# Causal mask added in the row maximum instead of by a matrix product, and small additions moved to GpSimd

## The chip, the cores and the metric

One core of a Trainium2 chip runs the whole kernel. The metric is the time on the device in microseconds (us), as the median of several executions. The engines work side by side, each through a queue of its own in order: TensorE (PE) multiplies matrices and writes to PSUM, VectorE (DVE) and ScalarE (ACT) read and write PSUM and SBUF, GpSimd (POOL) works on SBUF alone, and SyncE (SP) issues DMAs.

## What is computed

Causal attention over 2 batches and 12 heads of 448 positions and 64 dimensions, then a dense layer with squared ReLU, then a layer of 8 experts of which each token uses one. The change is in the attention:

```python
scores = scale * np.matmul(q, k.transpose(0, 1, 3, 2))
mask = np.triu(np.ones((seq, seq), dtype=bool), k=1)
scores = np.where(mask, -1000000000.0, scores)
scores = scores - np.max(scores, axis=-1, keepdims=True)
attn = np.exp(scores)
attn = attn / (np.sum(attn, axis=-1, keepdims=True) + 1e-09)
return np.matmul(attn, v).astype(np.float32)
```

## The kernel before

Attention works on 12 units, each a pair of heads of one batch. A unit's 448 queries are cut into 7 chunks of 64; a score tile holds the chunk's 64 queries of both heads on its 128 partitions, and the n = (c + 1) x 64 keys up to the chunk's end as columns, so that only its last 64 columns (QC) need a mask. There are 84 such tiles.

For each tile `s_scores` issues three products on PE (line 215; the operands are split into a high and a low part, kh and kl, q likewise) into one of four PSUM banks, then a fourth one (line 216): the identity matrix times `mask`, a tile of 0 and -1e9 in bf16, accumulated on the last 64 columns. Then DVE takes the negated row maximum `mn` (line 218), and ACT computes p = exp(s + mn) with the row sums `sm` as a by-product (line 219). The bank is free again when ACT has read it.

`s_norm` runs twice for each unit, for 4 chunks and for 3: DVE adds 1e-9 to the row sums (line 225) and takes the reciprocal `rs` (line 226), and POOL multiplies p by it (line 230). `s_trans` then transposes p on PE (line 247), ACT rounds the result to its high part (line 250, in the helper on line 59) and DVE subtracts to get the low part (line 251, in the helper on line 66). `s_pv` multiplies with v (line 264), and `s_x` stores the sum as xhi (ACT) and xlo (DVE). `s_prep` splits q and k of a later unit, and moves q into place with two DMAs from SP's queue (line 191).

The units run as a software pipeline: two steps for each unit, whose order of work is written out in `seq` (s is scores, n is norm, t is transpose, v is the product with v, p and w prepare a later unit). The tile framework turns that into a queue for each engine, ordered by a simulated timeline, and adds the semaphore waits; so a change of one instruction can shift others in their queues. In the first microseconds POOL fills the constants and clears the padding (lines 75 to 80, 145 to 151). Behind attention comes phase A (lines 288 to 290), the first dense layer, with 16 weight tiles that are loaded and converted by DVE, POOL and ACT on the way; the load of the first three hangs on the last row maximum issued so far (`last["max"]`).

Of the kernel before, what the change touches and what calls it, by code (L numbers as in the profile page):

```python
# [8 lines left out]
F32 = mybir.dt.float32  # L9
# [3 lines left out]
AF = mybir.ActivationFunctionType  # L13
ALU = mybir.AluOpType
AX = mybir.AxisListType
PSUM = bass.MemoryType.PSUM

B, H, S, D = 2, 12, 448, 64
NT, DM, FF = 896, 768, 2048
E, F = 8, 1024  # L20
P = 128
NP_ = H // 2
QC = 64
# [9 lines left out]
def f32(ap):  # L33
    return ap.bitcast(F32)


CFG = dict(
    first=1, rt5=[1, 3, 4, 5, 8], hp=3000, xe=[1, 10, 11, 12, 13], turn=5, xfd=[3, 4, 5, 6], xfj=[1, 2, 3, 4],
    joint=1, mhi="A", rt6=[1, 4, 7, 9, 15], woh="A", h2h="A", h2l="V", rt=[1, 3, 5, 7, 10], et=[9, 10, 14],
    turn2=[1, 3], ft0=[0, 1, 2, 3, 4], ft1=[3], ft2=[2, 4, 5, 6], ew=[2, 4, 10, 10, 10, 12, 14], stop=0, mlo="V", xh="A", h2="A",  # L40
    wh="G", wil="G", wol="GV", warm=6, nsa=6, nwi=3, nwb=3, wo0=4, hs0=[4, 5, 8, 9], conv0=17, convs=2, pin=1,
    qsb=2, pb=2, ptb=2, qkraw=3, vraw=2, vb=2, ss=4, pts=3, pvs=1, pas=4, wsp=1, mz="G",
    seq=("p0 s0 n0 t0 v0 s1 v1 s2 t1", "n0 t2 s0 v2 v3 t3 s1 s2 w0"),
    ch=(((2, 0, 1), (3,), ()), ((6,), (4, 5), ())), wn=[1], qh="A", qdir=1, qss=2, rpin=5, qdma="SS", kh="V",
    vh="AG", kl="G", vl="G", pth="AAAA", nrm="GGGGGGG", u0=1, order=[2, 1, 3, 0, 4])


def build(tc, qkd, vd, w_in, w_out, emb, tau, wm, cst, out, dbg_y=None):
    nc = tc.nc
    V, A, G, T, DMA = nc.vector, nc.scalar, nc.gpsimd, nc.tensor, nc.sync  # L50
# [20 lines left out]
    identb = cpool.tile([P, P], BF16, name="identb")  # L71
    V.tensor_copy(identb, ident)

    mask = cpool.tile([P, QC], BF16, name="mask")
# [54 lines left out]
    last = {}  # L129
    apool = tc.alloc_tile_pool(name="attn", bufs=1, side="right")  # L130
# [4 lines left out]
    units = [(b, pr) for b in range(B) for pr in range(NP_)]  # L135
# [8 lines left out]
    for i in range(Z):  # L144
# [5 lines left out]
        for x in vz[i] if i < len(vz) else ():  # L150
            ENG[CFG["mz"]].memset(f32(x[:, :, 1]), 0.0)

    def ab(key, u):
        x = CFG[key]
        return ENG[x[units.index(u) % len(x)]]
# [13 lines left out]
    def s_prep(u):  # L169

        d = st[u]
        for x in ("kh", "kl"):
            d[x] = apool.tile([P, S], F32R, tag=x, bufs=CFG["qsb"], name=x)
        d["q2"] = qz[units.index(u) % len(qz)]
        first = u == units[0] and CFG["u0"]
        copy_on(V if first else ab("kh", u), d["kh"], d["k"])

        def split(r, hi, lo):
            q = d["q"][r].rearrange("p (c a) -> p c a", a=QC)
            copy_on(ENG[CFG["qh"]], hi, q, scale=SCALE)  # L180
            V.scalar_tensor_tensor(out=lo, in0=q, scalar=SCALE, in1=f32(hi), op0=ALU.mult, op1=ALU.subtract)

        heads = [slice(h * D, (h + 1) * D) for h in range(2)]
        if units.index(u) < CFG["qdir"]:
            for h, r in enumerate(heads):
                split(r, d["q2"][r, :, h, :, 0], d["q2"][r, :, h, :, 1])
        else:
            q = apool.tile([P, NQ, QC, 2], F32R, tag="qs", bufs=CFG["qss"], name="qs")
            split(slice(0, P), q[:, :, :, 0], q[:, :, :, 1])
            for h, r in enumerate(heads):  # L190
                ENG[CFG["qdma"][h]].dma_start(out=f32(d["q2"][r, :, h]), in_=f32(q[r]))
        lo_of(V if first else ab("kl", u), d["kl"], d["k"], f32(d["kh"]))

    def s_prep_v(u):
        d = st[u]
        d["vh"], d["vl"] = vz[units.index(u) % len(vz)]
        vh, vl = (x[:, :, 0:3:2, :] for x in (d["vh"], d["vl"]))
        v = d["v"].rearrange("p a (h b) -> p a h b", h=2)
        copy_on(ab("vh", u), vh, v)
        lo_of(V if u == units[0] and CFG["u0"] else ab("vl", u), vl, v, f32(vh))  # L200
# [4 lines left out]
    def s_scores(u, c):  # L205

        d = st[u]
        if "p" not in d:
            for x in ("sm", "mn", "rs"):
                d[x] = apool.tile([P, NQ], F32, tag=x, bufs=3, name=x)  # L210
            d["p"] = pz[units.index(u) % len(pz)]
        n = (c + 1) * QC
        ss = ps_s.tile([P, 512], F32, tag="s", name="s")[:, 0:n]
        for i, (x, y) in enumerate(((0, "kh"), (0, "kl"), (1, "kh"))):
            T.matmul(ss, d["q2"][:, c, :, :, x].rearrange("p a b -> p (a b)"), d[y][:, :n], start=i == 0, stop=False)  # L215
        T.matmul(ss[:, n - QC:n], identb, mask, start=False, stop=True)  # L216
        i = COL[c]
        last["max"] = V.reduce_max(out=d["mn"][:, i:i + 1], in_=ss, axis=AX.X, negate=True)  # L218
        A.activation(d["p"][c][:, :n], ss, AF.Exp, bias=d["mn"][:, i:i + 1], accum_out=d["sm"][:, i:i + 1])  # L219

    def s_norm(u, cs):
        d = st[u]
        rs = d["rs"]
        x = slice(COL[cs[0]], COL[cs[-1]] + 1)
        V.tensor_scalar(out=rs[:, x], in0=d["sm"][:, x], scalar1=1.0e-9, scalar2=None, op0=ALU.add)
        V.reciprocal(rs[:, x], rs[:, x])
        for c in cs:
            p = d["p"][c][:, :(c + 1) * QC]
            if CFG["nrm"][c] == "G":
                G.tensor_scalar(out=p, in0=p, scalar1=rs[:, COL[c]:COL[c] + 1], scalar2=1.0, op0=ALU.mult, op1=ALU.mult)  # L230
            else:
                V.tensor_scalar(out=p, in0=p, scalar1=rs[:, COL[c]:COL[c] + 1], scalar2=None, op0=ALU.mult)
# [82 lines left out]
    def norm_at(k):  # L315
        u = (k + 2) // 2
        if 0 <= u < NU:
            s_norm(units[u], sum(CFG["ch"][k % 2], ()))
# [16 lines left out]
    for k in range(-3, 2 * NU + 2):  # L335
        u, h = divmod(k, 2)
        if h == 0 and -1 <= u and u + 3 < NU:
            s_load(units[u + 3])
        while len(wt) < min(NWI, max(0, (k - CFG["conv0"]) // CFG["convs"])):
            if CFG["pin"]:  # L340
                with tc.issue_after(last["max"].ins):
                    w_in_load()
            else:
                w_in_load()
        sc = scores_at(k)
        for x in CFG["seq"][h].split():
            i = int(x[1])
            if x[0] == "p" and -1 <= u and u + 2 < NU:
                s_prep(units[u + 2])
            if x[0] == "w" and 0 <= u + 1 < NU:  # L350
                s_prep_v(units[u + 1])
            if x[0] == "n":
                norm_at(k)
            if x[0] == "t" and 0 <= u < NU:
                s_trans(units[u], i)
            if x[0] == "v" and u >= 1:
                s_pv(units[u - 1], i)
                if i == NB - 1:
                    s_x(units[u - 1])
            if x[0] == "s":  # L360
                for y in sc[i]:
                    s_scores(*y)
                if k + 3 < len(CFG["wn"]):
                    warm(CFG["wn"][k + 3])
# [540 lines left out]
    y = ys[NTI - 1]  # L905
# [274 lines left out]
```

## Time and profile before

| | us |
|---|---|
| median of 3 runs | 587.28 |
| the runs | 587.99, 587.28, 583.95 |
| the profiled execution | 583.95 |
| its span, first to last instruction | 582.2 |

The profiled execution is the fastest of the three. PE is busy for 96% of the span and DVE for 69%. Rows give starts and durations; durations of neighbours on one engine overlap, so that the price of an instruction to its engine is read from start to start.

### The profile page before, as it was taken

To read this page: it belongs to the slowest core of one execution; us is meant where nothing else is said; L and a number is where in the kernel's file an instruction comes from. 1 tells how busy PE (TensorE), PEld (TensorE's weight loads), DVE (VectorE), ACT (ScalarE), POOL (GpSimd) and SP (SyncE) were. 2 spreads that over 40 slices of the span, in tenths; PEclk is the share of its full clock that TensorE was granted. 3 is DMA by queue.
4 is the path that set the end of the run, shared out by engine and by line. 5 is a ranking of instruction groups with operands and counts; after the bars stand their busy time and mean duration, and the time that the engine had idled before them with its cause. 6 is when DMAs were issued, how large, how long until landed. Compare 5 with 4: busy or idle time off the path is not lost.

```text
span 582.2 us, 9781 instructions
## 1 busy us (share of the span) xinstructions
PE 558.6 (96%) x3501; PEld 512.2 (88%) x3501; DVE 399.6 (69%) x901; ACT 291.5 (50%) x654; POOL 188.3 (32%) x204
## 2 busy tenths in 40 slices
PE   6999999999999999999999999899998999899994
PEld 3888788889999999999999999799997888799993
DVE  6878688955777878597664376975387986932641
ACT  4768678523343433434333226721478877923651
POOL 7676667854445544221000001001203412500010
PEclk8899999999999999999999999999999999899998
DMA  7757542223444655351000009404887987950310
GB/s 222 176 145 230 125 100 70 84 81 110 156 148 142 204 177 184 130 179 70 23 28 28 1 28 377 164 3 149 306 254 239 339 329 237 337 176 29 110 49 5
DMA packets 28233, 86.51 MB, mean 149 GB/s; under 512 B 2822, under 2 KB 13062, under 8 KB 28176
## 3 DMA queue, kind: packets, MB, share of 16 engines
q1 hardware_dynamic: 26640, 79.51, 42.3%
q0 software_dynamic: 1536, 6.29, 2.9%
q8 instruction: 29, 0.48, 0.3%
q14 instruction: 28, 0.23, 0.1%
HBM read 75.24 MB, written 6.29 MB: 140 GB/s over the span
## 4 chain that ended last, share of the span: by engine, by line
PE 85%; DVE 5%; DMA 4%; ACT 3%; issue 2%; SPq 1%; POOL 0%; POOLq 0%; ACTq 0%
PE yps L500 19%; PE ops L797 10%; PE pa L290 7%; PE pa L289 7%; PE pa L288 7%; PE pv L264 6%; PE s L215 5%; PE pt L247 3%; PE hps L707 3%; DMA q<-qs 3%; PE ops L739 3%; PE ops L734 2%; DVE ml L66 2%; PE hps L723 2%; PE hps L722 2%
## 5 line engine op out<-in xcount | busy, mean ns | idle before, releaser
L66 DVE TENSOR_TENSOR ml<-xraw,mh 128x768 fp32r<-128x768 f32 x64 | 60.1, 953 | 15.4 <-ACT mh L59 15.3
L59 ACT ACTIVATE mh<-xraw 128x768 fp32r<-128x768 f32 x64 | 53.3, 845 | 18.8 <-PE ops L734 9.3
L215 PE MATMUL s<-kh,q 128*128 128x128 f32 (+6 forms) x168 | 53.5, 352 | 4.3 <-ACT p L219 4.3
L797 PE MATMUL ops<-mh,act 128*128 128x384 f32 x224 | 53.5, 341 | 0.0
L819 POOL DMA_INDIRECT out<-osb,fsi x10 | 24.3, 2432 | 88.9 <-ACT osb L814 63.8
L230 POOL TENSOR_SCALAR p<-p,rs 128x192 f32<-128x192 f32 (+6 forms) x84 | 44.2, 545 | 17.9 <-ACT p L219 11.0
L264 PE MATMUL pv<-pt,v 128*128 128x448 f32 (+7 forms) x288 | 48.6, 303 | 0.2 <-DVE pt L66 0.2
L219 ACT ACTIVATE p<-s,mn 128x192 f32<-128x192 f32 (+6 forms) x84 | 39.5, 475 | 10.9 <-DVE mn L218 7.0
L123 DVE SCALAR_TENSOR_TENSOR w<-raw,w 128x768 int32<-128x768 int32 x32 | 42.8, 1339 | 0.7
L264 PEld LDWEIGHTS pv<-pt,v 128*128 128x128 f32 (+3 forms) x288 | 36.9, 163 | 5.4 <-issue 0.3
L215 PEld LDWEIGHTS s<-kh,q 128*128 128x128 f32 x168 | 35.5, 215 | 6.2 <-ACT p L219 4.9
L797 PEld LDWEIGHTS ops<-mh,act 128*128 128x128 f32 x224 | 39.2, 188 | 0.8
L66 DVE TENSOR_TENSOR ml<-mraw,mh 128x768 fp32r<-128x768 f32 x32 | 30.1, 953 | 14.3 <-ACT mh L59 14.3
L831 POOL DMA_INDIRECT xr<-ydram,fgi x10 | 10.7, 1067 | 89.3 <-DVE fsi L609 47.1
L66 DVE TENSOR_TENSOR hs<-h,hs 128x512 fp32r<-128x512 f32 (+1 forms) x32 | 21.9, 691 | 24.6 <-ACT hs L59 24.4
L218 DVE TENSOR_REDUCE mn<-s 128x1 f32<-128x192 f32 (+6 forms) x84 | 34.3, 415 | 5.7 <-PE s L216 5.5
L121 DVE SCALAR_TENSOR_TENSOR w<-raw,w 128x768 int32<-128x768 int32 x32 | 36.0, 1127 | 0.7
L294 ACT ACTIVATE relu<-pa 128x448 f32<-128x448 f32 x32 | 17.1, 537 | 36.3 <-PE pa L290 36.3
L119 DVE TENSOR_SCALAR w<-raw 128x768 int32<-128x768 int32 x32 | 22.2, 694 | 18.7 <-POOL wi3l L66 6.7
L66 DVE TENSOR_TENSOR pt<-pt 128x512 fp32r<-128x512 f32 x48 | 32.4, 680 | 3.1 <-ACT pt L59 3.1
L247 PE MATMUL pt<-ident,p 128*128 128x128 f32 x192 | 32.1, 284 | 0.0
L59 ACT ACTIVATE pt<-pt 128x512 fp32r<-128x512 f32 x48 | 28.1, 599 | 5.9 <-PE pt L247 3.8
(457 smaller groups left out, 1656.9 us busy)
## 6 DMA issues: line engine op xcount, KB each, us to landing
xraw<-in_wm SPq DMA_DIRECT2D x32, 768.0 KB, 6.3
raw<-in_w_in SPq DMA_DIRECT2D x16, 768.0 KB, 4.1
raw<-in_w_out SPq DMA_DIRECT2D x16, 768.0 KB, 4.2
mraw<-in_wm SPq DMA_DIRECT2D x16, 768.0 KB, 5.4
qk<-in_qkd SPq DMA_DIRECT2D x11, 448.0 KB, 4.8
q<-qs SPq DMA_DIRECT2D x22, 224.0 KB, 3.3
v<-in_vd SPq DMA_DIRECT2D x12, 256.0 KB
ydram<-ysb SPq DMA_DIRECT2D x7, 384.0 KB, 2.3
```

What stands on the lines that cost most here:

```text
L59: A.activation(out, in_, AF.Copy, scale=scale)
L66: eng.tensor_tensor(out=lo, in0=x, in1=hi, op=ALU.subtract)
L123: V.scalar_tensor_tensor(out=w[:, x], in0=raw[:, x, 0], scalar=29, in1=w[:, x], op0=ALU.logical_shift_right, op1=ALU.bitwise_or)
L215: T.matmul(ss, d["q2"][:, c, :, :, x].rearrange("p a b -> p (a b)"), d[y][:, :n], start=i == 0, stop=False)
L230: G.tensor_scalar(out=p, in0=p, scalar1=rs[:, COL[c]:COL[c] + 1], scalar2=1.0, op0=ALU.mult, op1=ALU.mult)
L247: T.transpose(pt[:, o * P:(o + 1) * P], d["p"][c][:, j * P:(j + 1) * P], ident)
L264: T.matmul(d["pv"][:, j * P:S] if h else d["pv"][0:D, j * P:S], d[x][0:k, j, 1:3].rearrange("p a b -> p (a b)") if h else d[x][0:k, j, 0], ...
L288: T.matmul(ps, wh[:, c], xhi[:, kc, gs], start=(kc == 0), stop=False)
L289: T.matmul(ps, wh[:, c], xlo[:, kc, gs], start=False, stop=False)
L290: T.matmul(ps, wl[:, c], xhi[:, kc, gs], start=False, stop=(kc == KC - 1))
L500: T.matmul(ps[t][c][:, :384], x, w[:, c * 384:(c + 1) * 384], start=(f == 0 and w is wh and x is hi), stop=(f == NF - 1 and x is lo))
L797: T.matmul(ps[c], x, ww[:, c * 384:(c + 1) * 384], start=(fc == 0 and x is hh and ww is wh), stop=(fc == 7 and x is hl))
```

## The change

All units but the first (`pm=1`) lose the product with the mask. A new tile `maskf` in f32 holds 384 columns of zeros and the mask behind them. DVE's new instruction adds its last n columns to the scores, negates the sum, writes it back to the PSUM bank, and takes the row minimum, which is the negated maximum `mn`; ACT computes exp(-1 x bank + mn). For these units the addition of 1e-9 goes from DVE to POOL; the reciprocal stays on DVE.

```diff
-    vh="AG", kl="G", vl="G", pth="AAAA", nrm="GGGGGGG", u0=1, order=[2, 1, 3, 0, 4])
+    vh="AG", kl="G", vl="G", pth="AAAA", nrm="GGGGGGG", u0=1, order=[2, 1, 3, 0, 4], pm=1)
...
+    maskf = apool.tile([P, S], F32, name="maskf")
+    G.memset(maskf[:, 0:S - QC], 0.0)
+    G.tensor_copy(maskf[:, S - QC:], mask)
...
+        first = units.index(u) < CFG["pm"]
         for i, (x, y) in enumerate(((0, "kh"), (0, "kl"), (1, "kh"))):
-            T.matmul(ss, d["q2"][:, c, :, :, x].rearrange("p a b -> p (a b)"), d[y][:, :n], start=i == 0, stop=False)
-        T.matmul(ss[:, n - QC:n], identb, mask, start=False, stop=True)
+            T.matmul(ss, d["q2"][:, c, :, :, x].rearrange("p a b -> p (a b)"), d[y][:, :n],
+                     start=i == 0, stop=i == 2 and not first)
         i = COL[c]
-        last["max"] = V.reduce_max(out=d["mn"][:, i:i + 1], in_=ss, axis=AX.X, negate=True)
-        A.activation(d["p"][c][:, :n], ss, AF.Exp, bias=d["mn"][:, i:i + 1], accum_out=d["sm"][:, i:i + 1])
+        mn = d["mn"][:, i:i + 1]
+        if first:
+            T.matmul(ss[:, n - QC:n], identb, mask, start=False, stop=True)
+            last["max"] = V.reduce_max(out=mn, in_=ss, axis=AX.X, negate=True)
+        else:
+            last["max"] = V.tensor_tensor_reduce(out=ss, in0=ss, in1=maskf[:, S - n:], scale=-1.0, scalar=3.0e38,
+                                                 op0=ALU.add, op1=ALU.min, accum_out=mn)
+        A.activation(d["p"][c][:, :n], ss, AF.Exp, bias=mn, scale=1.0 if first else -1.0,
+                     accum_out=d["sm"][:, i:i + 1])
...
-        V.tensor_scalar(out=rs[:, x], in0=d["sm"][:, x], scalar1=1.0e-9, scalar2=None, op0=ALU.add)
+        (V if units.index(u) < CFG["pm"] else G).tensor_scalar(out=rs[:, x], in0=d["sm"][:, x], scalar1=1.0e-9, scalar2=None, op0=ALU.add)
```

## Rows read from the trace of the kernel before

**Rows 1.** The page: its span, and busy us (share of the span) and instructions.

```profile
span 582.2 us, 9781 instructions
...
PE 558.6 (96%) x3501; PEld 512.2 (88%) x3501; DVE 399.6 (69%) x901; ACT 291.5 (50%) x654; POOL 188.3 (32%) x204
```

**Rows 2.** Busy us by stretch: PE, PEld, DVE, ACT, POOL; clock; DMA.

```profile
20.00:108.00 88.00, 86.88 (x664) 76.23 (x664) 70.66 (x180) 66.66 (x205) 59.82 (x95) 1.00 0.52 135
...
160.00:180.00 20.00, 20.00 (x101) 18.53 (x100) 14.76 (x13) 6.54 (x12) 9.39 (x6) 1.00 0.46 145
```

**Rows 3.** Waits, 12 to 112 us: waiter, releaser, us in total, times, longest.

```profile
ACT qs L59 <- DMA q<-qs: 11.7, 9, 3.1
...
POOL p L230 <- ACT p L219: 11.0, 5, 4.1
...
DVE mn L218 <- PE s L216: 5.5, 12, 1.0
PE s L215 <- ACT p L219: 4.3, 3, 3.4
```

**Rows 4.** Timeline of PE, two places: start, us, engine, line, operation.

```profile
97.25 0.28 PE L215 MATMUL s<-kh,q 128*128 128x256 f32 x1
97.37 0.20 PE L216 MATMUL s<-mask,identb 128*128 128x64 bf16 x1
97.41 0.46 PE L215 MATMUL s<-kh,q 128*128 128x448 f32 x1
97.70 0.36 PE L215 MATMUL s<-kl,q 128*128 128x448 f32 x1
97.90 0.37 PE L215 MATMUL s<-kh,q 128*128 128x448 f32 x1
...
86.03 0.31 PE L215 MATMUL s<-kh,q 128*128 128x128 f32 x1
86.18 0.28 PE L215 MATMUL s<-kl,q 128*128 128x128 f32 x1
86.30 0.28 PE L215 MATMUL s<-kh,q 128*128 128x128 f32 x1
```

**Rows 5.** DVE's groups by line and shape, 20 to 108 us: busy us, mean ns.

```profile
L181 DVE SCALAR_TENSOR_TENSOR qs<-qk,qs 128x448 fp32r<-128x448 f32 x8 | 6.9, 867 | 9.0 <-ACT qs L59 9.0
L218 DVE TENSOR_REDUCE mn<-s 128x1 f32<-128x448 f32 x11 | 6.8, 616 | 0.8 <-PE s L216 0.8
L66 DVE TENSOR_TENSOR xlo<-pv,xhi 128x448 fp32r<-128x448 f32 x9 | 5.6, 621 | 2.2 <-ACT xhi L59 2.0
```

**Rows 6.** Timeline of all engines, from 84 to 93.5 us.

```profile
87.58 1.71 POOL L230 TENSOR_SCALAR p<-p,rs 128x448 f32<-128x448 f32 x3
...
88.27 0.19 ACT L219 ACTIVATION_READ_ACCUMULATOR p<-s,mn 128x1 f32 x1
88.36 0.62 ACT L59 ACTIVATE v<-v 128x512 fp32r<-128x512 f32 x1
...
90.38 0.31 PE L247 MATMUL pt<-ident,p 128*128 128x128 f32 x1
...
91.11 0.16 DVE L225 TENSOR_SCALAR rs<-sm 128x4 f32<-128x4 f32 x1
91.18 0.49 DVE L218 TENSOR_REDUCE mn<-s 128x1 f32<-128x320 f32 x1
```

**Rows 7.** POOL's scaling of p by shape, 0 to 120 us: busy us, mean ns.

```profile
L230 POOL TENSOR_SCALAR p<-p,rs 128x448 f32<-128x448 f32 x12 | 8.4, 696 | 1.6 <-ACT p L219 1.1 <-DVE rs L226 0.5
...
L230 POOL TENSOR_SCALAR p<-p,rs 128x64 f32<-128x64 f32 x12 | 4.6, 384 | 0.0
```

**Rows 8.** Timelines of POOL and of DVE at the start, 0 to 25 us.

```profile
7.76 0.23 POOL L79 TENSOR_SCALAR_AFFINE_SELECT mask<-mask 64x64 bf16<-64x64 bf16 x1
9.16 1.13 POOL L66 TENSOR_TENSOR kl<-qk,kh 128x448 fp32r<-128x448 f32 x1 [1.16 <-DVE kh L61]
...
10.69 1.00 DVE L218 TENSOR_REDUCE mn<-s 128x1 f32<-128x192 f32 x4
```

## The prediction

> **What bounds the kernel now.** I read the page first, then the busy time by stretches, the waits, and last the timelines. TensorE (PE) is busy for 558.6 of 582.2 us [rows 1], so only work that PE does, or that PE waits for, can move the end. The change touches the attention stage alone. In 20 to 108 us, where that stage runs steadily, PE is busy 86.88 of 88.00 us at the full clock (1.00, which is 2.4 GHz); VectorE (DVE) has 70.66, ScalarE (ACT) 66.66 and GpSimd (POOL) 59.82 [rows 2]. The reader is to see two things there: PE is nearly full, and DVE comes second, at 80%. Because a busy PE is not PE at its peak, I also looked at who waits. PE's wait for a free score bank (its release by the exponential) comes to 4.3 us in three places, 3.4 of it in one. The others are those who wait: DVE's maximum waits 5.5 us for PE's mask product, ACT's split of q 11.7 us for a DMA [rows 3]. So PE's own issue sets the pace. Behind the stage, in 160 to 180 us, PE is busy 20.00 of 20.00 and DVE 14.76 [rows 2]: whatever attention ends earlier is handed on whole, because PE works through the next stage without a gap while the engine that converts its weights has a quarter of its time free.
>
> **The mask product that goes away.** Of 84 products on line 216, the seven of the first pair stay and 77 go. The timeline of PE gives the price by starts, since durations overlap. The last score product of 256 columns starts at 97.25, the mask product at 97.37, the next score product at 97.41: the mask product takes 0.04 us of its own [rows 4]. It also hurts its successor. That one, of 448 columns, lasts 0.29 us to the next start (97.41 to 97.70), while the next of the same width lasts 0.20 (97.70 to 97.90): 0.09 more. With 128 columns the successor lasts 0.15 against 0.12: 0.03 more [rows 4]. I read this as a weight load that a product of 64 columns is too short to cover. So one mask product costs between 0.04 us (nothing behind it is hurt) and 0.13 us. Its successors are score products of all widths, transposes of 128 columns and value products, most of them narrow; I take 0.075, between the 128-column successor (0.07) and the wide ones. The second pair's seven lie for the most part ahead of the stretch that PE fills, in the start-up that waits for loads, and I count nothing for them; 70 remain, so PE saves 70 x 0.075 = 5.3 us. The ends are 70 x 0.04 = 2.8 us and 77 x 0.13 = 10.0 us. The Trainium skill, "TensorE: Matmul & The Clock Gate", section "Back-to-back issue gap", gives N/2.4 + 2.5 ns for a product alone, about 29 ns for 64 columns and as an estimate 70 x 0.029 = 2.0 us, and says itself that short products cost more, since the formula has no room for their weight load; the trace agrees with that caution (0.04 us, and up to 0.09 behind it), and its rows carry the sum.
>
> **The maximum that now adds.** DVE's TENSOR_REDUCE becomes an instruction that reads the scores from PSUM and the mask from SBUF, writes the negated sum back to PSUM and yields the minimum as an accumulator. The trace has no such instruction. Its streaming part is bounded by the nearest row: the subtraction that makes xlo reads PSUM and SBUF at 448 elements in 621 ns, and the maximum over 448 takes 616 [rows 5]: no difference, as both go through one element at a time. An instruction with two SBUF operands costs more (the split of q: 867 ns mean for 448 elements [rows 5]), but the new one has only one operand there, like xlo, whose mean shows no stretching. What may be added is reading out the accumulator. Below, it is nothing: the row of a plain maximum already writes one number. Above, it is a second short instruction at full length, 0.19 us as ACT's read-out of its own accumulator shows (88.27); ACT starts the next instruction 0.09 us after it (88.36) [rows 6]. I take 0.09: a read-out that overlaps with what follows as short instructions do. In steady state DVE gains 70 x 0.09 = 6.3 us; the upper end is 70 x 0.19 = 13.3. The Trainium skill, "VectorE: DVE Perf Modes", section "Two Vector instructions with no wait between them", says that an operation which also writes its accumulator out is two instructions, an accumulator read behind the main one. No run here shows it on DVE; by that rule a read-out of some length is certain, and nothing at all is out of the range.
>
> **The small additions that move.** Of 24 additions of 1e-9 on line 225, two (the first pair) stay on DVE and 22 go to POOL. One costs DVE 0.07 us by starts (91.11 to 91.18 [rows 6]), so DVE loses 20 x 0.07 = 1.4 us of steady work. On POOL the scaling of p costs 384 ns for 64 columns and 696 for 448 [rows 7]; the line through the two leaves 0.33 us for 4 columns, an estimate, 20 x 0.33 = 6.6 us for an engine that has 28 us free. The reciprocal stays on DVE, so the chain becomes ACT's sums, POOL, DVE, POOL, with some 0.3 to 0.5 us more to the first scaled p. The cover is the time between scaling and transposing: the three p that POOL starts at 87.58 are finished at 89.29, and the transposes that need them begin at 90.38, 1.1 us later [rows 6]. Where that cover is gone, PE waits for the difference. The new wait is at DVE's reciprocal: behind it in DVE's queue stand maxima and the subtractions of pt, and for these ACT and PE wait. POOL idles today for ACT's p, 11.0 us in five places [rows 3]; there the addition finds POOL free.
>
> **Start-up.** POOL gets a memset of 384 columns and a copy of 64 more. POOL is done with the old mask at 7.76 + 0.23 = 7.99 us, then waits 1.16 us for DVE; and the first maximum runs at 10.69, when POOL has been done with the mask for 2.7 us [rows 8]. About 0.7 us more on POOL (as long as one scaling of 448 columns [rows 7]) lies in that gap. I count nothing; uncovered it would cost 0.7 us, once.
>
> **The sum.** DVE in 20 to 108 us: 70.66 + 6.3 - 1.4 = 75.6 us, against 88.0 - 5.3 = 82.7 for PE: 91%, below PE, so PE still sets the pace and the saving is 5.3 us. The profiled execution took 583.95 us (its span 582.2 and 1.75 around it) and would come to 578.7; it is the fastest of the three, and the median is 587.28. Measured against the median I predict 587.3 - 5.3 = 582.0.
>
> **The rivals.** (1) DVE becomes the bound. With the read-out at 0.19, DVE has 70.66 + 13.3 - 1.4 = 82.6 us of work against PE's 82.7, and in-order queues cannot both be full; if a third of DVE's 17.3 us of idle time now stays, the stretch takes 82.6 + 5.8 = 88.4, no gain, about 587.7. It decides from a read-out of about 0.11 us, where 70.66 + 7.7 - 1.4 + 5.8 reaches PE's 82.7; the forecast's 0.09 is close to it. For it: DVE is the second-fullest engine and each of its additions is in line; against it: xlo and the maximum cost the same, and ACT's read-outs cost it 0.09. (The Trainium skill's rule above, two instructions for one, is on this rival's side.) (2) Slower: DVE's reciprocal waits for POOL. If POOL's queue puts the addition behind a subtraction for kl or v, DVE stands still for up to the length of such a one, 1.13 us [rows 8]; 20 times 1.1 is 22 us on DVE, with the 6.3 and the -1.4 that is 70.7 + 26.9 = 97.6, 9.6 over the 88 of today: about 597. The wait decides from about 0.6 us each (70.66 + 4.9 + 12 = 87.6). Against it: POOL mostly waits for the sums already. A milder form, 0.8 us each, gives 70.66 + 4.9 + 16 = 91.6, 3.6 over today's 88: 591. (3) More is saved: the mask product at its upper price with 70 of them is 70 x 0.13 = 9.1 us: 578.2. For it: wide successors do show 0.13; against: many are narrow, and DVE at 75.6 of 78.9 would hardly follow. (4) The saved time is given back: the q transfers, which ACT waits 11.7 us for [rows 3], do not get shorter when PE does, so ACT's exponentials stand behind them longer, and PE waits for a score bank. Against it: that wait is only 4.3 us today [rows 3]. Half of the gain lost gives 584.6.
>
> **How the numbers follow.** The forecast 0.40; rival 4, a part of the gain, 0.15; rival 1, no gain, 0.20; rival 2 0.13; rival 3 0.12. Faster by over 1% means under 581.4, and slower over 593.2; 1% is about what a measurement of this kernel can tell from no change, the three runs lie 0.7% apart. The forecast itself spreads over 579.5 to 584.5, and half of it lies under 581.4 when the price and the scatter of the runs are taken together: 0.40 x 0.5 + 0.12 + 0.03 of rival 4 = 0.35. Slower: the full form of rival 2, 0.08 of its 0.13. Within 1%: 0.57. The range leaves out rival 2 (0.13) and the far end of rival 3 (0.05): 576.5 to 589.5.
>
> **What would show it.** Right: in the changed profile line 216 has 7 products, PE in the attention stretch stays over 95% busy, the stretch is some 5 us shorter, the successors of 448 columns lose their 0.09 us, and the new maximum over 448 stays under 0.75 us. Rival 1 shows as DVE over 95% busy with PE waiting for ACT's p, and a read-out row near 0.19 us. Rival 2 shows as DVE's reciprocal waiting for POOL's addition. Wrong altogether would be a stage after 120 us that changes by as much as attention: the order of its instructions would have moved, which no row of before can tell.

## The result, and the profile after

The changed kernel takes 579.51 us (median of 4 runs, 578.43 to 580.77) against 587.63 us before (4 runs, 583.95 to 588.06): a ratio of 0.9876, 95% interval 0.9831 to 0.9921, or 7.3 us less (4.6 to 9.9). Timed again on another chip it was 0.9903 (0.9871 to 0.9935), 5.7 us less. Differences in us are taken from the ratios; a ratio is an estimate of its own from the runs and can differ from the quotient of the two medians by up to 0.2% (here that quotient is 0.9862, or 8.1 us). The forecast of 582.0 us, 5.3 us less, lies inside both. The two profiled executions, 583.95 and 578.43 us, lie 5.5 us apart. One profile read below, of the kernel with the change for all units (592.66 us), is of a slow execution, at a granted clock of 0.82 instead of 1.00 from 20 to 40 us; its rows are used only up to 20 us, where its clock is 0.75 as in the changed kernel.

First the page of the changed kernel (span; busy us, share and instructions) and its busy time by stretch, which answer to [rows 1, 2]:

```profile
span 576.7 us, 9694 instructions
...
PE 552.8 (96%) x3424; PEld 509.6 (88%) x3424; DVE 397.5 (69%) x956; ACT 290.8 (50%) x654; POOL 197.1 (34%) x228
```

```profile
20.00:102.00 82.00, 81.35 (x589) 74.02 (x588) 68.67 (x229) 65.71 (x203) 63.31 (x112) 1.00 0.53 137
```

PE does 77 instructions fewer and is busy for 5.8 us less. The steady stretch is some 6 us shorter, so it ends near 102 us, and PE is as full in it as before (99%). Where the time was won shows in the first and last starts of the value products, which end attention. Before, then after (count, least/median/most ns, first to last start in us):

```profile
L264 PE MATMUL pv<-pt,v x288: 219/307/453, 24.2 to 130.2; 128*64 128x320 f32 x36, 128*64 128x192 f32 x36, 64*64 64x64 f32 x36, 128*64 128x448 f32 x24
```

```profile
L279 PE MATMUL pv<-pt,v x288: 219/307/455, 23.7 to 124.4; 128*64 128x320 f32 x36, 128*64 128x192 f32 x36, 64*64 64x64 f32 x36, 128*64 128x448 f32 x24
```

The last one starts 5.8 us earlier, the first one only 0.5: the gain grows over the attention stage and not in the start-up. The same kind of rows has the second layer's first product, with the weight wo0h, at 239.6 before and 233.6 after (6.0 earlier), and the last experts' product at 573.7 and 567.8 (5.9). So it was handed on whole.

What became of the mask products shows in PE's timeline, which answers to [rows 4]:

```profile
83.88 0.28 PE L221 MATMUL s<-kl,q 128*128 128x256 f32 x1
84.00 0.49 PE L221 MATMUL s<-kh,q 128*128 128x256 f32 x2
84.33 0.36 PE L221 MATMUL s<-kl,q 128*128 128x448 f32 x1
84.53 0.37 PE L221 MATMUL s<-kh,q 128*128 128x448 f32 x1
84.74 0.49 PE L262 MATMUL pt<-ident,p 128*128 128x128 f32 x3
84.98 0.40 PE L221 MATMUL s<-kh,q 128*128 128x320 f32 x1
85.22 0.31 PE L221 MATMUL s<-kl,q 128*128 128x320 f32 x1
85.37 0.31 PE L221 MATMUL s<-kh,q 128*128 128x320 f32 x1
```

The row at 84.00 is two products: the last of 256 columns and, with no mask product between them, the first of 448. Both together last 0.33 us to 84.33; 0.12 for 256 columns leaves 0.21 for the 448 columns, where 0.29 stood in [rows 4]. The successor got its 0.09 back, or nearly. The rows below show that a transpose of 128 columns does the same harm: the first product of 320 columns behind transposes lasts 0.24 (84.98 to 85.22), the next one 0.15. That price stays.

The prediction read the harm as a weight load that is not covered. The rows of the weight loads (PEld) bear this out. Around the 448 columns that start at 97.41 before [rows 4], then behind the 448 columns that start at 84.12 after:

```profile
97.37 0.21 PEld L215 LDWEIGHTS s<-kh,q 128*128 128x128 f32 x1
97.50 0.20 PEld L215 LDWEIGHTS s<-kl,q 128*128 128x128 f32 x1
```

```profile
84.12 0.20 PEld L221 LDWEIGHTS s<-kl,q 128*128 128x128 f32 x1
```

In both kernels the next product starts some 0.2 us after the start of its load (97.50 to 97.70, 84.12 to 84.33). After the change that load starts together with the product of 448 columns; behind the mask product it starts 0.09 us later, and the load of the 448 columns themselves began only at 97.37, with the mask product. Over the stage, 67 of the 73 mask products from 20 us on can be compared with the same kind of successor in the changed kernel: by medians of the starts, the mask product takes 0.04 us of its own and its successor 0.04 more, 0.08 in all.

The new maximum in DVE's timeline and in its groups of 0 to 120 us (busy us, mean ns), which answers to [rows 5]:

```profile
84.67 0.14 DVE L231 DVE_READ_ACCUMULATOR2_ANT mn<- 128x1 f32 x1
84.67 0.62 DVE L66 TENSOR_TENSOR xlo<-pv,xhi 128x448 fp32r<-128x448 f32 x1
...
85.20 0.62 DVE L231 CUSTOM_DVE_ANT_0 s<-s,maskf 128x448 f32<-128x448 f32 x1
...
85.74 0.14 DVE L231 DVE_READ_ACCUMULATOR2_ANT mn<- 128x1 f32 x1
85.74 0.69 DVE L66 TENSOR_TENSOR pt<-pt 128x512 fp32r<-128x512 f32 x1
```

```profile
L231 DVE CUSTOM_DVE_ANT_0 s<-s,maskf 128x448 f32<-128x448 f32 x11 | 6.9, 627 | 1.1 <-PE s L221 1.1
...
L240 POOL TENSOR_SCALAR rs<-sm 128x3 f32<-128x3 f32 x11 | 3.4, 305 | 1.0
...
L240 POOL TENSOR_SCALAR rs<-sm 128x4 f32<-128x4 f32 x11 | 3.3, 296 | 3.3 <-PE pt L262 1.8 <-PE s L221 0.6 <-ACT p L233 0.4
```

The instruction takes 627 ns for 448 columns, the plain maximum took 616. Behind it there is a read-out row of 0.14 us; but the next instruction starts in the very moment in which the read-out does (84.67 and 84.67, 85.74 and 85.74). From 85.20 to 85.74 are 0.54 us for the maximum of 448 columns; the plain maximum took 0.53 by starts. The next instruction starts with the read-out behind 52 of the 73 read-outs from 20 us on; behind nearly all the others DVE had to wait for something first. The read-out costs DVE no time.

The waits of 12 to 112 us, which answer to [rows 3]:

```profile
POOL p L245 <- DVE rs L241: 10.8, 8, 2.7
ACT qs L59 <- DMA q<-qs: 10.6, 8, 2.3
...
DVE s L231 <- PE s L221: 3.2, 7, 1.1
...
PEld s L221 <- ACT p L233: 2.4, 7, 0.7
...
DVE rs L241 <- POOL rs L240: 0.6, 1, 0.6
...
PE s L221 <- ACT p L233: 0.5, 1, 0.5
```

POOL's wait for ACT's p has turned into a wait for the reciprocal, of the same length; POOL has the time. DVE waited for POOL's addition once, 0.6 us.

### The profile page after: what moved, and what is told of

Same layout as the page of the kernel before. It is cut to its first block, busy times and chain, and to the rows that moved or that the text cites. A ratio compares the mean times of both kernels' runs of the same rounds, so it can differ in the third digit from the quotient of the medians.

```text
span 576.7 us, 9694 instructions
## 1 busy us (share of the span) xinstructions
PE 552.8 (96%) x3424; PEld 509.6 (88%) x3424; DVE 397.5 (69%) x956; ACT 290.8 (50%) x654; POOL 197.1 (34%) x228
## 4 chain that ended last, share of the span: by engine, by line
PE 82%; DVE 6%; ACT 4%; DMA 3%; issue 2%; SPq 0%; POOL 0%; POOLq 0%; ACTq 0%; DVEq 0%
PE yps L515 19%; PE ops L812 8%; PE pa L303 7%; PE pa L305 7%; PE pa L304 7%; PE pv L279 7%; PE s L221 5%; DVE ml L66 3%; PE pt L262 3%; PE hps L722 3%; PE hps L738 2%; PE hps L737 2%; PE hps L739 2%; PE ops L754 2%; PE ops L749 2%
## 5 line engine op out<-in xcount | busy, mean ns | idle before, releaser
L221 PE MATMUL s<-kh,q 128*128 128x128 f32 (+6 forms) x168 | 52.0, 347 | 3.0 <-ACT p L233 2.6
L279 PE MATMUL pv<-pt,v 128*128 128x448 f32 (+7 forms) x288 | 49.9, 304 | 0.0
L245 POOL TENSOR_SCALAR p<-p,rs 128x192 f32<-128x192 f32 (+6 forms) x84 | 42.5, 525 | 11.2 <-DVE rs L241 10.8
L846 POOL DMA_INDIRECT xr<-ydram,fgi x10 | 14.9, 1490 | 88.3 <-DVE fsi L624 47.0
L123 DVE SCALAR_TENSOR_TENSOR w<-raw,w 128x768 int32<-128x768 int32 x32 | 43.1, 1350 | 0.7
L119 DVE TENSOR_SCALAR w<-raw 128x768 int32<-128x768 int32 x32 | 24.2, 755 | 20.3 <-POOL wi3l L66 7.3
L121 DVE SCALAR_TENSOR_TENSOR w<-raw,w 128x768 int32<-128x768 int32 x32 | 34.5, 1080 | 0.7
L231 DVE CUSTOM_DVE_ANT_0 s<-s,maskf 128x192 f32<-128x192 f32 (+6 forms) x77 | 31.8, 430 | 3.7 <-PE s L221 3.2
```

Of the source, the lines that this page charges most:

```text
L123: V.scalar_tensor_tensor(out=w[:, x], in0=raw[:, x, 0], scalar=29, in1=w[:, x], op0=ALU.logical_shift_right, op1=ALU.bitwise_or)
L279: T.matmul(d["pv"][:, j * P:S] if h else d["pv"][0:D, j * P:S], d[x][0:k, j, 1:3].rearrange("p a b -> p (a b)") if h else d[x][0:k, j, 0], ...
```

## The experiments

Theory A is the prediction's: the gain is the time of the mask products on PE, and what was put on DVE and POOL is hidden. Theory B: DVE is near its bound, so that taking the additions off it is part of the gain. Theory C: the framework orders the queues anew for each kernel, and the gain came with that order. Ratios are to the kernel before, timed on the same chip (medians of 584.9 to 585.8 us in these runs), with 95% intervals.

**The additions.** Kept on DVE:

```diff
-        (V if units.index(u) < CFG["pm"] else G).tensor_scalar(out=rs[:, x], in0=d["sm"][:, x], ...
+        V.tensor_scalar(out=rs[:, x], in0=d["sm"][:, x], ...
```

> The change with all small additions kept on DVE. Theory A (the gain is the time of the 77 mask products on PE, and everything that was put on DVE and POOL is hidden): the same as the changed kernel, 0.988 of before within 0.2%, about 579.5 us. Theory B (DVE is near its bound, so taking 1.4 us of additions off it is part of the gain): 1.4 us or more slower than the changed kernel, 581 us and up.

Measured: 579.41 us, 0.9902 (0.9871 to 0.9933). As that was another chip than the changed kernel's, both ran again side by side:

> The changed kernel itself, timed on the same chip as the three kernels beside it. Theory A: about 0.988 of before.

> The change with the additions kept on DVE, a second time, beside the changed kernel on one chip. Theory A: the two agree within 1 us. Theory B (moving the additions is part of the gain): 1.4 us or more slower than the changed kernel. Seen so far on another chip: 0.990 of before against the changed kernel's 0.988.

Measured: the changed kernel 579.64 us, 0.9903 (0.9871 to 0.9935); with the additions on DVE 579.34 us, 0.9899 (0.9868 to 0.9930). And the additions moved alone, with nothing else changed:

> The kernel before with only the small additions of all units but the first moved to POOL; products and maxima as before. Theory A: as before, within 1 us of 587. Theory B: 1.4 us or more faster than before. The prediction's rival 2 (DVE's reciprocal waits for POOL): slower than before by 4 us or more.

Measured: 584.93 us, 0.9994 (0.9973 to 1.0015). The three agree: moving the additions to POOL gives and costs nothing that these runs can tell. (The interval of the last reaches from 1.6 us less to 0.9 more, so that Theory B's 1.4 us is unlikely rather than excluded by it alone.) The prediction's rival 2, 4 us slower or more, is gone. One more thing can be read here: the first run of the additions-on-DVE kernel has its last value product at 126.0 us, the second run of the same kernel at 123.6. A single profile of this stage is good to about 2.4 us. Of this difference 1.7 us stands in PE's waits: those of over 0.1 us from 20 to 130 us add to 2.5 us in the first and 0.8 in the second.

**The products.** Kept on PE, with the new maximum as well:

```diff
-                     start=i == 0, stop=i == 2 and not first)
+                     start=i == 0, stop=False)
+        T.matmul(ss[:, n - QC:n], identb, mask, start=False, stop=True)
...
-            T.matmul(ss[:, n - QC:n], identb, mask, start=False, stop=True)
```

> The mask product kept on PE for all units and the new maximum on DVE as well (the mask is added twice, which changes no output), additions on DVE. Theory A: PE's work is that of before, so the time is that of before, 587 within 1.5 us, and no faster. Rival 1 (the new maximum costs DVE 0.09 us or more each and DVE is near its bound): 3 us or more slower than before. Theory C (the gain came with the new order of the queues or with the new maximum itself): faster than before by half of the gain or more, under 583.5.

Measured: 586.67 us, 1.0029 (1.0003 to 1.0055), 1.7 us slower than before. With the products on PE there is no gain at all, so it was not the new maximum as such. Theory A said "no more than 1.5". In the profile PE waits 2.7 us from 20 to 130 us, against 1.1 before, nearly all of it for score banks; that is about the difference, and one profile cannot tell whether the maximum or the new order of the queues made it.

The product doubled:

```diff
+        if u != units[0]:
+            T.matmul(ss[:, n - QC:n], identb, mask, start=False, stop=False)
         T.matmul(ss[:, n - QC:n], identb, mask, start=False, stop=True)
```

> The kernel before with the mask product issued twice for all units but the first, which changes no output: 77 products more on PE. Theory A: the time rises by what the change took away or somewhat less, as the second product follows a short one: 77 x 0.04 to 0.08, 3 to 6 us, to 590 to 593. Theory C: no change in proportion, 587 within 2 us.

Measured: 589.7 us, 1.0069 (1.0042 to 1.0096), 4.0 us more (2.5 to 5.6). PE's timeline of this kernel:

```profile
60.26 0.20 PE L217 MATMUL s<-mask,identb 128*128 128x64 bf16 x1
60.30 0.19 PE L218 MATMUL s<-mask,identb 128*128 128x64 bf16 x1
60.33 0.28 PE L215 MATMUL s<-kh,q 128*128 128x64 f32 x1
```

By starts the first product takes 0.04 us, as before, and the second one 0.03; its successor is hurt already. So 77 x 0.03 = 2.3 us is PE's own price, just under the interval. The rest shows as waiting: ACT's split of q waits 4.02 us for a DMA and starts at 43.80, exponentials stand behind it, and PE waits 1.84 us for a score bank, up to 45.34. The time rises with the number of products, as theory A has it, but not by their price alone.

The product taken away without anything put in its place:

```diff
...
-        T.matmul(ss[:, n - QC:n], identb, mask, start=False, stop=True)
+        if u == units[0]:
+            T.matmul(ss[:, n - QC:n], identb, mask, start=False, stop=True)
```

> The kernel before without the mask product for all units but the first, and with the plain maximum: the causal mask of these units is left out, so the scores, the routing behind them and the last layers differ, and only the attention stretch can be compared. Theory A (DVE's new work is hidden): attention's last value product ends within 1 us of the changed kernel's 124.6 us. If DVE's new maximum costs something on the way, it ends 2 us or more earlier, 122.6 us or less.

Measured: the last value product starts at 126.4 us, against 124.4 in the changed kernel (123.8 in its second profile). That is not within the 1 us that Theory A gave, but within the 2.4 us of one profile, and it is not earlier. (Its whole time, 652.66 us, says nothing: other tokens go to other experts.) PE waits 3.5 us from 20 to 130 us in this kernel and 0.6 in the changed one, so its later end is waiting, and the run does not decide what the new maximum costs. That it costs about what a plain one does rests on the rows above (0.54 against 0.53 us by starts).

Half of the units (`pm=6`):

> The change for the last six units only, so 42 of the 77 products go. Theory A: 42/77 of the gain, 0.55 x 7.3 = 4.0 us, about 583.3 us or 0.993 of before. Theory C (order of the queues): no such proportion; all of the gain or none.

Measured: 583.94 us, 0.9969 (0.9935 to 1.0002), 1.8 us less (at most 3.8). The 4.0 us that was expected from the first ratio lies just outside. Taken from the gain of 1.0% that the later runs agree on, 42/77 would be 0.9945, and inside. The run excludes all of the gain (0.9903); none of it lies just inside the interval. So it fits a part of the gain and does not prove one.

Taken together: no kernel that keeps the products gains, and two kernels without them, the changed one and the one with the additions on DVE, gain the same 1.0% with queues that differ. Theory C is left without support as the source of the gain; that the order of the queues can take the gain away again shows in the runs that follow.

**DVE's room.** The prediction had counted on DVE carrying 0.09 us more for each maximum. It did not have to; would it have been hidden? A short instruction ahead of each new maximum:

```diff
+            junk = apool.tile([P, 1], F32, tag="junk", bufs=2, name="junk")
+            V.reduce_max(out=junk, in_=ss[:, n - QC:n], axis=AX.X, negate=True)
             last["max"] = V.tensor_tensor_reduce(...
```

> The changed kernel with one more short instruction on DVE ahead of each of the 77 new maxima: the maximum of the tile's last 64 columns, whose result nobody reads; about 0.12 us each by starts, 9 us on DVE in all, somewhat more than the read-out of 0.09 us that the prediction had assumed. Theory A as predicted (DVE has room): at most 2 us slower than the changed kernel. If DVE's time counts in full: 9 us slower, slower than before.

Measured: 587.06 us, 1.0014 (0.9991 to 1.0037), which is 6.5 us more than the changed kernel. The whole gain is gone. Then the same amount of work hung on nothing, reading the mask tile instead of the scores and put behind the maximum:

```diff
+            junk = apool.tile([P, 1], F32, tag="junk", bufs=2, name="junk")
+            V.reduce_max(out=junk, in_=maskf[:, S - QC:], axis=AX.X, negate=True)
```

> The changed kernel with 77 short instructions more on DVE as in the run before, but of work that hangs on nothing and that nothing waits for (the maximum of 64 columns of the mask tile), so that the scores do not wait for them directly. If what cost 7 us in that run was only the longer way from scores to exponential: within 2 us of the changed kernel, 0.990 to 0.994 of before. If DVE's queue has no room for 9 us more, wherever it stands: 4 us or more slower than the changed kernel, 0.997 or more.

Measured: 584.27 us, 0.9986 (0.9966 to 1.0006), 4.9 us more than the changed kernel. The time falls in the second branch, whose reason was that DVE's queue has no room. The busy times do not bear that reason out. First the kernel with the work behind the maximum, from 20 to 60 and from 60 to 100 us, then the changed kernel in the same stretches:

```profile
20.00:60.00 40.00, 35.98 (x243) 31.05 (x243) 34.38 (x141) 29.37 (x93) 25.98 (x47) 0.99 0.58 160
60.00:100.00 40.00, 39.79 (x290) 36.55 (x289) 34.19 (x137) 30.46 (x95) 31.54 (x57) 1.00 0.43 110
```

```profile
20.00:60.00 40.00, 39.87 (x288) 36.22 (x287) 34.31 (x116) 32.93 (x104) 30.39 (x56) 1.00 0.65 182
60.00:100.00 40.00, 39.48 (x289) 35.83 (x288) 32.57 (x107) 30.79 (x95) 30.91 (x54) 1.00 0.39 92
```

From 60 to 100 us DVE is busy for 34.2 of 40.0 us, 85%, with the additional work, and PE does as much as in the changed kernel (290 and 289 products) and waits 0.2 us in all. The loss lies in the first half, where PE stands still for 4.0 us; yet the changed kernel has the same DVE time there, 34.3 us, beside a PE that is full. The waits of the kernel with the work behind the maximum, 12 to 112 us, and the longest of PE's waits behind 20 us:

```profile
PE s L221 <- ACT p L235: 5.5, 5, 2.6
PEld s L221 <- ACT p L235: 5.4, 9, 1.7
...
ACT p L235 <- DVE rs L243: 2.4, 3, 1.0
...
ACT p L235 <- DVE mn L231: 2.4, 6, 0.6
```

```profile
26.14 0.61 ACT L59 ACTIVATE qs<-qk 128x448 fp32r<-128x448 f32 x1 [1.31 <-DMA q<-qs]
...
27.08 0.42 PE L221 MATMUL s<-kh,q 128*128 128x320 f32 x1 [1.30 <-ACT p L235]
```

PE waits for score banks 5.5 us, where the changed kernel has 0.5; 2.6 of it lies ahead of 20 us. The wait at 27.08 follows a split of q that stands ahead of exponentials in ACT's queue and waited for a DMA; from 20 to 60 us these waits of ACT add to 6.6 us, in the changed kernel to 4.5. With the work ahead of the maximum the loss is spread more evenly: PE waits 2.7 us from 20 to 60 us, 1.7 from 60 to 100 and 1.2 behind that.

So both runs show that 77 short instructions more on DVE can undo the gain, wherever they stand, and neither shows that DVE's load as such did it. How much is the load and how much the order of the queues, which the framework makes anew when instructions are added, stays open.

**The first pair.** The change for all 12 units (`pm=0`):

> The change for all 12 units, the first too: the last seven products go. They lie in the start-up, which waits for loads and runs at half clock. Theory A: within 0.7 us of the changed kernel, 579 to 580. If the first unit's maximum is made to wait for the mask tile that POOL fills last, slower than the changed kernel by up to 1 us.

Measured: 586.43 us, 1.0008 (0.9974 to 1.0043). Not 1 us lost, but the whole gain. Its timelines of POOL, DVE, ACT and PE in the start-up (what stands in brackets is the idle time before, and what ended it):

```profile
11.33 0.64 POOL L156 CAST maskf<-mask 128x64 f32<-128x64 bf16 x1
...
12.00 0.37 DVE L231 CUSTOM_DVE_ANT_0 s<-s,maskf 128x192 f32<-128x192 f32 x1
...
15.73 0.60 ACT L59 ACTIVATE qs<-qk 128x448 fp32r<-128x448 f32 x1 [4.52 <-DMA q<-qs]
16.35 0.42 ACT L233 ACTIVATE p<-s,mn 128x192 f32<-128x192 f32 x1
...
16.92 0.74 PE L221 MATMUL s<-kh,q 128*128 128x448 f32 x1 [9.17 <-ACT p L233]
```

and the same places in the changed kernel:

```profile
9.99 1.00 DVE L228 TENSOR_REDUCE mn<-s 128x1 f32<-128x192 f32 x4
...
10.37 0.42 ACT L233 ACTIVATE p<-s,mn 128x192 f32<-128x192 f32 x1
...
10.93 0.74 PE L221 MATMUL s<-kh,q 128*128 128x448 f32 x1 [2.14 <-ACT p L233]
```

With the first pair on the new path, DVE's first maximum waits for the mask tile, which POOL finishes at 11.97 behind two conversions: 2 us. In ACT's queue the third split of q now stands ahead of the first exponential, and waits 4.52 us for a DMA; the exponentials stand behind it, and PE's score banks behind them. A delay of 2 us became 6 (16.92 against 10.93). To test the first half of that, the tile was built directly in f32, ahead of POOL's clearing of the padding (the bf16 mask and the small identity, which nothing reads any more, go):

```diff
+    maskf = apool.tile([P, S], F32, name="maskf")
+    V.memset(maskf[:, 0:S - QC], 0.0)
+    for i in range(P // QC):
+        m = maskf[i * QC:(i + 1) * QC, S - QC:]
+        G.memset(m, 0.0)
+        G.affine_select(out=m, in_=m, pattern=[[-1, QC]],
+                        compare_op=ALU.is_ge, fill=NEG, base=0, channel_multiplier=1)
...
-    G.tensor_copy(maskf[:, S - QC:], mask)
```

> The change for all 12 units, with the mask tile built directly in f32 ahead of POOL's other start-up work (additions of the first pair on DVE, as in the change). With the tile late, the change for all units was no faster than before: its first new maximum began at 12.00 us, when POOL had just finished the tile, and PE then waited 9.2 us for a score bank. If the late tile and the queue order that came with it cost that, the first maximum now begins at 10.0 us or earlier and the time is that of the changed kernel or up to 1 us better, 0.986 to 0.988. If it is the new maximum on the first pair as such, as slow as before, 0.997 or more.

Measured: 583.49 us, 0.9973 (0.9950 to 0.9995). The first maximum starts at 10.40 us (10.0 or earlier was expected) and PE's products go on at 11.63, against 16.92 with the late tile: in the start-up 5.3 of the 6.0 us are back. Of the time it is a third by the ratios, 2.0 of 6.1 us, and the intervals of the two runs overlap; the time itself falls in the branch "as slow as before". In this kernel the split of q that waits for a DMA stands ahead of exponentials later on:

```profile
33.42 0.60 ACT L59 ACTIVATE qs<-qk 128x448 fp32r<-128x448 f32 x1 [3.86 <-DMA q<-qs]
33.92 0.29 ACT L221 ACTIVATE p<-s,mn 128x64 f32<-128x64 f32 x1
...
34.35 0.48 PE L215 MATMUL s<-kh,q 128*128 128x448 f32 x1 [1.00 <-ACT p L221]
```

PE's waits from 20 to 100 us add to 3.9 us, against 0.6 in the changed kernel. So the rows show the late tile as the cause of the late start. That the rest of the loss is this order of ACT's queue is what the rows suggest; no run shows it alone, and the new maximum on the first pair as such is not excluded. Neither kernel beats the change, and the first pair does well to keep its mask product.

## Why the prediction was right, and where only its sum was

**PE sets the pace: right.** PE stays at 99% of its stretch, and the time goes with the number of products: none gained with the products kept (1.0029), 4.0 us lost with twice as many, some 2.3 of it by their own price.

**The price of a mask product: right.** 70 x 0.075 = 5.3 us was forecast; the last value product comes 5.8 us earlier, 0.5 of it because PE waits less (1.1 us before, 0.6 after, from 20 to 130 us), and the timed gains are 5.7 to 7.3 us. The successor's part is there: 448 columns take 0.21 instead of 0.29 us, and over the stage a product comes to 0.08 us, 0.075 forecast. Without the successor, at 0.04 us each, the sum would have been 2.8 us, below every timed interval of the whole change. One small term was put at nothing too early: the second pair's seven mask products start at 16.2 to 21.6 us, and PE is busy 5.00 of 5.00 us from 15 to 20; the first value product comes 0.5 us earlier.

**The streaming part of the new maximum: right.** 627 against 616 ns.

**The read-out: mis-sized.** Forecast 0.09 us on DVE with 0.19 as the upper end; it is an instruction of 0.14 us that takes no time of DVE, since the next one starts along with it. The prediction held nothing at all to be out of the range because there are two instructions; there are two, and nothing was still the right end. The size did not enter the saving, only the check whether DVE gets in PE's way. ACT's read-out, the nearest row, misled, as it does hold up what follows it.

**DVE's room: not put to the test, and here the hit is partly luck.** The sum put DVE at 75.6 of 82.7 us (91%) and concluded that PE still sets the pace. Measured, DVE has 68.7 of 82.0 us (84%), because the read-out is free, so the case that the forecast reckoned with did not arise. The runs that did put some 0.13 us more on DVE for each maximum lost 6.5 and 4.9 us of the gain: with a read-out of 0.09 us the change might have gained little, rival 1's case. The step that these runs put in doubt is the one that compares busy times. DVE's maxima stand between PE's products and the exponential that frees PE's bank, and a sum over the stretch leaves out when each of them comes: the same 34.3 us of DVE in 40 stood beside a full PE and beside one that waited 4.0 us.

**The additions: right.** POOL's addition took 0.30 us (0.33 forecast), DVE waited for it 0.6 us once, and the runs give it none of the gain that they can tell. The cover became thinner: where the transposes came 1.1 us behind the last scaled p [rows 6], one such place has 0.42 us now (scaled from 84.04 for 1.70 us, transposed at 86.16):

```profile
84.04 1.70 POOL L245 TENSOR_SCALAR p<-p,rs 128x448 f32<-128x448 f32 x3 [0.31 <-DVE rs L241]
...
86.16 0.27 PE L262 MATMUL pt<-ident,p 128*128 128x128 f32 x1
```

**The start-up: right for this change, and its price without cover wrong.** Nothing was lost, as the first pair does not read the new tile. "Uncovered it would cost 0.7 us" was far too little: in the run for all units the first maximum came 2 us late and PE 6.

**Handed on: right.** 5.8 us at the end of attention, 6.0 at the start of the second layer, 5.9 at the last experts' product. Rival 4, the gain given back to the q transfers, did not come about; ACT's wait for them is 10.6 us, 11.7 before. Its mechanism shows all the same in other kernels: in the one for all units and in the one with two mask products, a long wait of PE (9.17 and 1.84 us) stands behind a split of q that waited more than 4 us for a DMA.

## What to carry to other kernels

A short product can cost more than its columns, here because the weight load behind it starts late: count it from the start of one neighbour to the start of the one after next. Busy shares do not tell whether a second engine has room when its results free the first one's buffers. Look at the waits of the full engine and at what stood ahead in the queue of whatever released it; add a small dummy load and see whether the time moves, and remember that the dummy also moves the order of the queues. And what a start-up hides should be priced by what stands behind it in each queue, not by its own length.

## What the runs showed of the hardware

DVE's read-out of an accumulator is a row of 0.14 us of its own, and the next instruction starts at the same time (behind 52 of 73; behind nearly all the others DVE had to wait). An addition and a row minimum in one instruction, PSUM and SBUF in, PSUM and one column out, cost DVE what the plain maximum did (627 and 616 ns for 448 columns, 0.54 and 0.53 us by starts). A transpose of 128 columns hurts a wide product behind it as the 64-column product did: 0.24 us for 320 columns, 0.15 for the next. Behind the 64-column product the weight load after next starts 0.09 us late (at 97.50, not with the product at 97.41), and the product that needs it starts 0.2 us after that.
